# Three PSUM tiles that take turns from chunk to chunk, and an early copy of the fourth product

## The chip, the cores and the metric

The kernel runs on one core of one Trainium2 chip. The metric is the device time of one execution in microseconds (us); the time before is the median of three runs. The profile is of one further execution, whose own time is given beside its span.

The engines are called as the profile calls them: PE (matmuls), PEld (PE's weight loads, which overlap its matmuls), DVE, ACT, POOL, and SP, which only issues transfers.

## The reference, cut to what matters

One transformer block on `x` of 2048 tokens by 576, all in fp32:

```python
h  = x + attention(layernorm(x)) @ wo        # 32 heads of 18, window of 8 keys, dilation 2
n  = layernorm(h)
g  = n @ w_gate                              # 576 x 4608
u  = n @ w_up                                # 576 x 4608
out = h + (sigmoid(g) * u) @ w_down          # 4608 x 576
```

The change touches only the way in which `g` and `u` leave PSUM. What is computed stays the same.

## The kernel before, in words

**Blocks and chunks.** The tokens are cut into four blocks of 512. The 4608 columns of `w_gate` and `w_up` are cut into 36 chunks of 128. A product of one chunk is a PSUM tile of 128 columns by 512 tokens, which is one whole bank of 2 KB per partition. fp32 values are split into a high and a low part (`split`, lines 103 to 105: ACT copies the high part, DVE subtracts), and each product is made of three passes: high by high, weight high by operand low, weight low by operand high.

**Two ways to do a chunk.** A list of 86 items (line 971) is worked off in order. In the first way, `single` (line 644), one block's `g` and `u` are computed plainly with the PSUM tiles `b1` and `b2`. In the second, `pair` (line 671), two blocks are done together, and seven products take the place of eight (the scheme of Strassen and Winograd; the operands `s1` to `s4` and `t1` to `t4` are sums and differences made before). The order of items is: 14 `single` for block 0, 22 `pair` for blocks 0 and 1, 14 `single` for block 2, 36 `pair` for blocks 2 and 3. The text counts items from 0, so the first `pair` stage is items 14 to 35 and the second is items 50 to 85.

**One chunk of `pair`.** The seven products are called product 1 to product 7 here. A product is six matmuls with 512 columns (`prod`, line 604, matmuls on line 609), and products 2, 5, 6 and 7 have two more for the last 64 rows of the contraction (`rest`, line 613, matmuls on line 616).

| product | tile before | what follows it |
|---|---|---|
| 1: `a00` by `b00` | `b1`, fresh | ACT copies it to `s1` (line 676) |
| 2: `a01` by `b10` | `b2`, fresh | DVE adds it to `s1` (681), ACT takes the sigmoid (682): gate of the first block |
| 3: `s2` by `t2` | `b1`, added to product 1 | ACT copies the sum to `s2` (686) |
| 4: `s3` by `t3` | `b3`, fresh | nothing yet |
| 5: `s1` by `t1` | `b1`, added on | ACT copies the sum to `s3` (693), then DVE adds `b3` to `s3` (694): up of the second block |
| 6: `a11` by `t4` | `b3`, added to product 4 | DVE adds it to `s2` (699), ACT takes the sigmoid (700): gate of the second block |
| 7: `s4` by `b11` | `b1`, added on | `last`: DVE multiplies the first gate by `b1`, then the second gate by `s3` (line 629, or 1041 in the second pair stage) |

Product 6 writes on `b3` and so must come after line 694 has read it. Product 3 of each chunk must come after line 676, and product 5 after line 686. Product 1 of the next chunk takes `b1` afresh, and so must come after the multiplication by `b1`. `s1` to `s3` come from four buffers that take turns (`s_tile`, line 632).

**The other work of those stages.** `between(0)` to `between(6)` stand behind the products. They let in the down projection, which runs a few items behind: in the first pair stage 24 matmuls with 288 columns after products 5 and 7 (`down_units`, matmuls on line 719), in the second stage one step of six such matmuls after each product (`down_seven`, matmuls on line 781, each step's PSUM tile copied out by ACT on line 787 and added to DRAM by POOL's queue on line 790). The last four chunks go back to the plain scheme (`down_tail`, line 756). The first pair stage also has the attention of blocks 2 and 3 behind it, which is DVE work in pieces such as line 182. Weights are split one chunk ahead (`weights`, line 575).

**PSUM.** The eight banks are `b1`, `b2`, `b3`, `bgp`, and two tiles `dp` of two banks each, which take turns. The projections that run under the `single` items use `b3` and `bgp` (`bg_bank`, line 640).

**What sets the order.** Each engine works through its own list in order. The lists are made when the program is built, by a planner of the framework that simulates the engines with its own estimates. It takes the instruction that it thinks ready first, and among ready ones the one with the higher priority, then the one that was traced first. So the order on PE can differ from the program's text: where the planner thinks a product is blocked, it lets matmuls of the down projection go ahead. `tc.high_priority(HC)` raises the priority of the evictions (copies and adds that read PSUM). A new tile on a bank waits until every reader and writer of the tile before it is done.

Of the kernel before, what the change touches and what calls it, by code (L numbers as in the profile page):

```python
# [17 lines left out]
AF = mybir.ActivationFunctionType  # L18
ALU = mybir.AluOpType
# [34 lines left out]
HC = 700  # L54
# [6 lines left out]
def kernel(ctx, tc, x, wqkv, wo, wmlp, out):  # L61
    nc = tc.nc
    dve, act, pool, pe, sp = nc.vector, nc.scalar, nc.gpsimd, nc.tensor, nc.sync
# [540 lines left out]
    def prod(ps, xx, w, n, first):  # L604
        wt, k0 = w[n]
        k = 0
        for c in range(2):
            for a, m in ((0, 0), (0, 2), (1, 0)):
                pe.matmul(ps, wt[:, a, k0 + c], xx[:, m + c], start=first and k == 0,  # L609
                          stop=k == 5, skip_group_check=True)  # L610
                k += 1

    def rest(ps, xx, w, n):
        wt, k0 = w[n]
        for a in range(2):
            pe.matmul(ps, wt[:, a, k0], xx[:, 4], start=False, stop=a == 1,  # L616
                      skip_group_check=True)
# [14 lines left out]
    def s_tile():  # L632
        return gh.tile([P, TB], F32, tag="s", bufs=4, name="s")

    def b_tile(i):
        return gp.tile([P, TB], F32, name=f"b{i % 3 + 1}")
# [31 lines left out]
    added = [None]  # L668
    gated = [None]

    def pair(X, w, between, last):
        b1, b2, b3 = b_tile(0), b_tile(1), b_tile(2)
        s1, s2, s3 = s_tile(), s_tile(), s_tile()
        prod(b1, X["a00"], w, "b00", True)
        with tc.high_priority(HC):
            act.activation(s1, b1, AF.Copy)
        between(0)
        prod(b2, X["a01"], w, "b10", True)
        rest(b2, X["a01"], w, "g4")
        with tc.high_priority(HC):  # L680
            added[0] = dve.tensor_tensor(s1, s1, b2, ALU.add)
            act.activation(s1, s1, AF.Sigmoid)
        between(1)
        prod(b1, X["s2"], w, "t2", False)
        with tc.high_priority(HC):
            act.activation(s2, b1, AF.Copy)
        between(2)
        prod(b3, X["s3"], w, "t3", True)
        between(3)
        prod(b1, X["s1"], w, "t1", False)  # L690
        rest(b1, X["a11"], w, "u4")
        with tc.high_priority(HC):
            act.activation(s3, b1, AF.Copy)
            added[0] = dve.tensor_tensor(s3, s3, b3, ALU.add)  # L694
        between(4)
        prod(b3, X["a11"], w, "t4", False)
        rest(b3, X["a11"], w, "g4")
        with tc.high_priority(HC):
            added[0] = dve.tensor_tensor(s2, s2, b3, ALU.add)
            gated[0] = act.activation(s2, s2, AF.Sigmoid)  # L700
        between(5)
        prod(b1, X["s4"], w, "b11", False)
        rest(b1, X["s4"], w, "u4")
        with tc.high_priority(HC):
            last((s1, b1), (s2, s3))
        between(6)
# [253 lines left out]
    def units(n):  # L960
        for _ in range(n):
            while queue:
                if next(queue[0], END) is END:
                    queue.pop(0)
                else:
                    break
# [139 lines left out]
    for c, (kind, p, f) in enumerate(items):  # L1106
# [26 lines left out]
        def last(h0, h1):  # L1133
            hid[0] = hidden(*h0, "h0")
            hid[1] = hidden(*h1, "h1")
# [3 lines left out]
        elif not by_seven:  # L1139
            side = last_pair if c == NF - 1 else bg_step  # L1140

            def between(i):
                if i in (4, 6):
                    units(2)
                side(i)

            pair(X, w, between, last)
        else:
            def between(i):
# [12 lines left out]
                down_side(f, i)  # L1162

            pair(X, w, between, last if f >= NF - NPL else last_sums(f))
            if f < NF - NPL:
                if f % 2:
# [57 lines left out]
```

## Time and profile before

| what | us |
|---|---|
| time, median of three runs (lowest, highest) | 1599.83 (1598.15, 1600.38) |
| time of the profiled execution | 1598.48 |
| its span | 1596.1 |
| PE busy | 1561.0 (98% of the span) |
| weight loads | 1381.9 (87%) |
| DVE busy | 1269.6 (80%) |
| ACT busy | 875.3 (55%) |
| POOL busy | 184.0 (12%) |

The span lies between the first and the last instruction, and 2.4 us of the profiled execution's time lie around it. Busy time counts overlapping instructions once. Matmuls overlap, so a row of a matmul group shows a duration that is longer than the step from one matmul to the next; what one matmul costs is the step between starts. A wait of PE is shown twice: at the matmul, and at the weight load (PEld) ahead of it.

### The profile page before, as it was taken

Reading aid. Unit: us, or ns where it says so; the run is one execution under the profiler, and the core shown is the slowest. Engines: PE = TensorE matmul, PEld = TensorE weight load, DVE = VectorE, ACT = ScalarE, POOL = GpSimd, SP = SyncE. Lnnn points to the kernel's source line nnn. Section 1 sums busy time; section 2 is a strip of 40 time slices with the busy share of each in tenths; the row PEclk is TensorE's granted clock in tenths of the full one; section 3 lists DMA queues with packets and bytes.
Section 4 is the critical chain, followed back from the end, with each engine's and each line's share of the span. In section 5 each row is a group of like instructions: output and inputs, shape, how many; then the busy total and the mean of one; then the engine's idle time right before and its main releaser. Section 6 shows DMA issues by size and latency. Waiting matters only on the chain.

```text
span 1596.1 us, 22354 instructions
## 1 busy us (share of the span) xinstructions
PE 1561.0 (98%) x8532; PEld 1381.9 (87%) x8532; DVE 1269.6 (80%) x1931; ACT 875.3 (55%) x1546; POOL 184.0 (12%) x230
## 2 busy tenths in 40 slices
PE   7999979999999999999999999999999999999998
PEld 6999968798888888888989988888888888888887
DVE  7999989859999999999446777876777776677755
ACT  5432234435565566566443345766777776677751
POOL 1000000011000010001001100112112112211110
PEclk9999999999999999999999999999999999999999
DMA  7654544446466666666754234888888889888983
GB/s 270 205 203 168 187 183 165 154 162 247 112 167 186 163 161 168 169 176 153 200 185 164 78 111 123 186 182 177 170 171 188 175 168 183 172 167 181 187 166 123
DMA packets 76891, 273.50 MB, mean 171 GB/s; under 512 B 8336, under 2 KB 14224, under 8 KB 75888
## 3 DMA queue, kind: packets, MB, share of 16 engines
q0 software_dynamic: 27792, 105.89, 35.0%
q1 hardware_dynamic: 41360, 146.06, 27.8%
q10 hardware_dynamic: 7632, 20.12, 3.3%
q8 instruction: 67, 1.10, 0.3%
q14 instruction: 40, 0.33, 0.1%
HBM read 145.88 MB, written 128.52 MB: 172 GB/s over the span
## 4 chain that ended last, share of the span: by engine, by line
PE 83%; DVE 9%; DMA 4%; issue 1%; ACT 1%; POOL 0%; SPq 0%; DVEq 0%; POOLq 0%; ACTq 0%
PE b L609 40%; PE dp L719 14%; PE dp L781 11%; PE b L616 7%; PE acc L150 5%; DMA wg<-in_wmlp_dram 1%; PE b L150 1%; PE bgp L150 1%; DVE pr L182 1%; DVE pr L208 1%; DVE lg L186 1%; DVE w L105 1%; DMA x<-tok 1%; DVE tl L105 1%; DMA ar<-x 1%
## 5 line engine op out<-in xcount | busy, mean ns | idle before, releaser
L609 PE MATMUL b<-tl,w 128*128 128x512 f32 x1716 | 441.4, 396 | 8.7 <-ACT w L104 6.2
L609 PEld LDWEIGHTS b<-tl,w 128*128 128x128 f32 x1716 | 310.3, 189 | 68.8 <-ACT w L104 7.3
L609 PE MATMUL b<-th,w 128*128 128x512 f32 x1368 | 355.0, 394 | 1.0 <-DVE s L694 0.5
L609 PEld LDWEIGHTS b<-th,w 128*128 128x128 f32 x1368 | 248.7, 188 | 54.1 <-DVE s L694 4.7
L616 PE MATMUL b<-th,w 128*128 128x512 f32 x572 | 176.4, 390 | 0.0
L104 ACT ACTIVATE w<-wg 128x640 fp32r<-128x640 f32 (+2 forms) x197 | 116.5, 597 | 107.9 <-PE b L616 40.2
L790 POOL DMA_DIRECT2D h<-ev x128 | 110.1, 862 | 464.6 <-ACT ev L787 446.2
L787 ACT ACTIVATE ev<-dp 128x576 f32<-128x576 f32 x224 | 144.8, 647 | 34.0 <-PE dp L781 31.1
L150 PE MATMUL acc<-qw,th 128*128 128x432 f32 x512 | 155.8, 365 | 1.1 <-DVE th L109 0.8
L105 DVE TENSOR_TENSOR w<-wg,w 128x640 fp32r<-128x640 f32 (+2 forms) x197 | 126.6, 649 | 37.0 <-ACT w L104 36.7
L105 DVE TENSOR_TENSOR w<-tw,w 128x512 fp32r<-128x512 f32 x116 | 79.6, 687 | 70.0 <-ACT w L104 69.0
L616 PEld LDWEIGHTS b<-th,w 128*128 128x128 f32 x572 | 107.4, 188 | 22.7
L104 ACT ACTIVATE w<-tw 128x512 fp32r<-128x512 f32 x116 | 73.3, 632 | 91.1 <-PE b L609 85.7
L719 PE MATMUL dp<-d,h0h 128*128 128x288 f32 x640 | 119.3, 296 | 0.9 <-DVE tail L729 0.9
L719 PE MATMUL dp<-d,h1h 128*128 128x288 f32 x640 | 120.2, 297 | 0.0
L719 PEld LDWEIGHTS dp<-d,h0h 128*128 128x128 f32 x640 | 99.6, 190 | 5.0 <-DVE tail L729 1.2
L150 PEld LDWEIGHTS acc<-qw,th 128*128 128x128 f32 x512 | 97.2, 190 | 6.5 <-DVE th L109 1.1
L719 PEld LDWEIGHTS dp<-d,h1h 128*128 128x128 f32 x640 | 99.6, 190 | 2.9 <-ACT h1h L104 0.2
L150 PE MATMUL acc<-qw,tl 128*128 128x432 f32 x256 | 92.8, 362 | 0.0
L384 ACT ACTIVATE ev<-acc 128x432 f32<-128x432 f32 x64 | 33.9, 531 | 104.9 <-PE acc L153 101.7
L727 ACT ACTIVATE stage<-dp 128x576 f32<-128x576 f32 x96 | 61.8, 646 | 40.3 <-PE dp L719 40.0
L182 DVE TENSOR_TENSOR pr<-kw,q 128x2304 f32<-128x2304 f32 x32 | 81.7, 2552 | 2.7 <-DMA kw<-k 2.6
(278 smaller groups left out, 2904.5 us busy)
## 6 DMA issues: line engine op xcount, KB each, us to landing
h<-ev POOLq DMA_DIRECT2D x96, 576.0 KB, 7.0
wg<-in_wmlp_dram SPq DMA_DIRECT2D x49, 928.0 KB, 5.1
h<-stage POOLq DMA_DIRECT2D x24, 1152.0 KB, 11.1
wg<-in_wmlp_dram SPq DMA_DIRECT2D x36, 640.0 KB, 4.9
kw<-k SPq DMA_DIRECT2D x16, 792.0 KB, 4.3
vw<-v SPq DMA_DIRECT2D x16, 792.0 KB, 5.4
wd<-in_wmlp_dram SPq DMA_DIRECT2D x18, 576.0 KB, 6.6
h<-ev POOLq DMA_DIRECT2D x32, 288.0 KB, 6.1
```

Source lines behind the costliest of these rows:

```text
L104: act.activation(hi, src, AF.Copy)
L105: splits.append(dve.tensor_tensor(lo, src, f32(hi), ALU.subtract))
L150: pe.matmul(ps[:, :n], a[:, c, js], m[:, c], start=k == 0, stop=False)
L182: dve.tensor_tensor(pr, both(kw, u), q[:, us].unsqueeze(2).broadcast_to([P, 2, W, CG]), ALU.mult)
L384: act.activation(ev[:, :, j], ps[:, :NQ].rearrange("p (t c) -> p t c", t=3), AF.Copy)
L609: pe.matmul(ps, wt[:, a, k0 + c], xx[:, m + c], start=first and k == 0, stop=k == 5, skip_group_check=True)
L616: pe.matmul(ps, wt[:, a, k0], xx[:, 4], start=False, stop=a == 1, skip_group_check=True)
L719: pe.matmul(ps[:, i, :DH2], a[:, js], d[:, m, i * DH2:(i + 1) * DH2], start=k == 0, stop=k == n)
L727: act.activation(hv, ps, AF.Copy)
L781: pe.matmul(ps[:, i, :DH2], a[x][:, js], m[y], start=k in (0, 1, 3) and q == 0, stop=q == 2, skip_group_check=True)
L787: act.activation(hs[:, k % 2], ps[:, :, :DH2], AF.Copy)
L790: pool.dma_start(hsev[:, u, k0:k + 1], hs[:, :k + 1 - k0], accum_op=ALU.add, max_dma_last_dim=8 * D)
```

## The change: what it does

Before, `pair` always takes the tiles `b1`, `b2`, `b3` in this order. After, a counter `turn` goes up by one with each chunk, and the three tiles are taken from that place on: `b1, b2, b3`, then `b2, b3, b1`, then `b3, b1, b2`, and so on (`b_tile` takes its number modulo three). The names in the code keep their parts: what the code calls `b1` holds products 1, 3, 5 and 7.

Beside this the up sum of the second block is put together the other way round. Before, ACT copied the tile of products 1, 3 and 5 to `s3` after product 5, and DVE added the tile of product 4. After, ACT copies the tile of product 4 to `s3` as soon as product 4 is done, and DVE adds the tile of products 1, 3 and 5 after product 5. The number of instructions of each kind is the same.

```diff
+    turn = [2]
+
     def pair(X, w, between, last):
-        b1, b2, b3 = b_tile(0), b_tile(1), b_tile(2)
+        turn[0] += 1
+        b1, b2, b3 = (b_tile(turn[0] + k) for k in range(3))
         s1, s2, s3 = s_tile(), s_tile(), s_tile()
...
         prod(b3, X["s3"], w, "t3", True)
+        with tc.high_priority(HC):
+            act.activation(s3, b3, AF.Copy)
         between(3)
         prod(b1, X["s1"], w, "t1", False)
         rest(b1, X["a11"], w, "u4")
         with tc.high_priority(HC):
-            act.activation(s3, b1, AF.Copy)
-            added[0] = dve.tensor_tensor(s3, s3, b3, ALU.add)
+            added[0] = dve.tensor_tensor(s3, s3, b1, ALU.add)
         between(4)
         prod(b3, X["a11"], w, "t4", False)
```

## The prediction

> **What bounds the kernel now.** I read the page first, then PE's waits, then PE's busy time and clock by stage, and last the chain of waits and the timeline inside the second pair stage. From the page, and from the table of waits of PE over the whole span (total us, times, longest):
>
> ```profile
> span 1596.1 us, 22354 instructions
> PE 1561.0 (98%) x8532; PEld 1381.9 (87%) x8532; DVE 1269.6 (80%) x1931; ACT 875.3 (55%) x1546; POOL 184.0 (12%) x230
> ```
> ```profile
> PE bgp L139 <- DVE tl L105: 3.9, 1, 3.9
> PE b L609 <- DVE s L629: 2.9, 2, 2.5
> ...
> PE b L609 <- DVE s L694: 0.5, 1, 0.5
> ```
>
> PE is the bound, and the table shows one wait on line 694, of 0.5 us. By that table the change has almost nothing to win. But it lists gaps between matmuls only, and a late weight load hides in the matmul's own duration. The weight loads' waits inside the second pair stage (1009.77 to 1527.7 us), and the windows of PE's busy time (columns: window, its length, PE, PEld, DVE, ACT, POOL, PE clock, DMA share, GB/s):
>
> ```profile
> PEld b L609 <- DVE s L694: 2.9, 16, 0.2
> ```
> ```profile
> 819.50:826.30 6.80, 5.89 (x22) 5.37 (x23) 5.38 (x11) 4.69 (x11) 0.00 (x0) 0.50 0.39 146
> 1009.77:1527.70 517.93, 517.93 (x2760) 449.13 (x2759) 374.90 (x645) 369.74 (x646) 102.55 (x120) 1.00 0.89 179
> ```
>
> PE is busy for all of 517.93 us, yet 16 weight loads wait for line 694, some 0.2 us each. What such a wait costs is read from the pitch. The chain of waits in that stage (start, length, what) is PE alone, and repeats every 34.53 us, which is two chunks with the 14 steps of the down projection between:
>
> ```profile
> 1013.49 0.45 PE b L616 x2
> 1013.94 1.46 PE dp L781 x11
> 1015.40 1.60 PE b L609 x6
> 1017.01 0.45 PE b L616 x2
> 1017.46 0.13 PE dp L781
> 1017.59 1.37 PE b L609 x6
> 1018.96 0.45 PE b L616 x2
> 1019.41 0.94 PE dp L781 x7
> 1020.35 1.48 PE b L609 x6
> 1021.83 0.66 PE dp L781 x5
> 1022.50 1.37 PE b L609 x6
> ...
> 1031.32 1.59 PE dp L781 x12
> 1032.91 1.65 PE b L609 x7
> ...
> 1037.93 1.45 PE b L609 x6
> ...
> 1048.47 1.46 PE dp L781 x11
> ```
>
> Six undisturbed matmuls of line 609 take 1.37 us (product 7 at 1017.59, product 2 at 1022.50), so one costs 0.228; a matmul of line 781 costs 0.133 (1.46 by 11). Directly after down matmuls I allow 1.39 for six: 0.02 for the change of shape. Four pieces take longer than that. The one at 1015.40 is product 6, the one at 1020.35 the next chunk's product 1, the one at 1032.91 begins with product 6 of the second chunk, and the one at 1037.93 is product 1 of the chunk after. From the timeline of all engines, what these wait for:
>
> ```profile
> 1013.98 0.60 ACT L693 ACTIVATE s<-b 128x512 f32<-128x512 f32 x1 [1.19 <-PE b L616]
> ...
> 1014.61 0.69 DVE L694 TENSOR_TENSOR s<-s,b 128x512 f32<-128x512 f32 x1 [1.85 <-ACT s L693]
> ...
> 1015.35 1.22 PEld L609 LDWEIGHTS b<-th,w 128*128 128x128 f32 x6 [0.18 <-DVE s L694]
> ...
> 1019.45 0.69 DVE L1041 TENSOR_TENSOR r<-s,b 128x512 f32<-128x512 f32 x1
> ```
>
> Product 5 ends, ACT copies its tile, DVE then adds `b3`, and only at 1015.30 may product 6 write `b3`. PE had pulled five matmuls of the next down step forward (11 in a row at 1013.94, not 6) and still came too early. Likewise line 1041 reads `b1` until 1020.14, and product 1 at 1020.2 is the new tile on that bank.
>
> **The change part by part.**
>
> *The early copy.* No instruction is added or removed; the 0.60 us copy moves from product 5's end to product 4's, and the 0.69 us add stays where it was. Product 6 now waits for the copy of product 4's tile, which has all of product 5 and a down step as cover: 8 x 0.228 + 0.8 = 2.6 us against 0.60. So product 6's waits go. Per two chunks: 1.60 - 1.38 = 0.22 us, and 1.65 - 7 x 0.229 = 0.05.
>
> *What it newly makes late.* Product 7 adds to the tile that DVE now reads after product 5, so it waits for line 694. Its cover runs from product 5's end to product 7's start, 1013.94 to 1017.59 = 3.65 us in the rows, against 0.69 of add; DVE work of up to 2.9 us may stand ahead of the add before PE feels it. On ACT, the copy waits for product 4; behind it are queued evictions of the down projection and weight splits, which waited in the same way behind product 5 before, so this trades places and costs nothing while ACT keeps up (369.74 of 517.93 us busy). `s3` is held longer by some 2.6 us; its buffer was the last chunk's `s2`, whose last reader, the second multiplication of line 1041 right behind the one at 1019.45, is done three products before product 4 ends. No transfer moves; SP and POOL have the same lists.
>
> *The turn.* Product 1 now takes the bank that the last chunk's product 2 had, free since line 681, a whole half chunk earlier. Its wait for line 1041 goes: 1.48 - 1.39 = 0.09 and 1.45 - 1.39 = 0.06 per two chunks, call it 0.16 with rounding. Product 2 takes the bank that line 699 reads with an add like line 694's of 0.69 us right after product 6; from there to product 2 lie product 7, a down step and product 1, 1.82 + 0.8 + 1.37 = 4.0 us. Product 4 takes the bank of line 1041, later still. Nothing binds there.
>
> *Sum in the second stage.* 0.22 + 0.05 + 0.16 = 0.43 us per two chunks, with the rounding of the rows 0.40 to 0.48; I take 0.44. 32 of the 36 chunks carry the seven-product down projection (the table's 16 waits are one per two chunks): 16 x 0.44 = **7.0 us**. As an upper bound: two chunks have 100 matmuls of lines 609 and 616 and 14 x 6 = 84 of line 781, and 100 x 0.228 + 84 x 0.133 = 33.97 us of bare matmuls against the period of 34.53 leave 0.56, so no more than 9.0 us even if every change of shape became free.
>
> *First pair stage: nothing.* Its 22 chunks show no wait of these kinds, since a full down tile pair stands there after product 5 (these rows are from the chain over the whole span and from the page's groups):
>
> ```profile
> 395.33 3.18 PE dp L719 x24
> ```
> ```profile
> L182 DVE TENSOR_TENSOR pr<-kw,q 128x2304 f32<-128x2304 f32 x32 | 81.7, 2552 | 2.7 <-DMA kw<-k 2.6
> ```
>
> *The border to the second stage.* Items 50 on start at another place of the turn (22 chunks are one more than a multiple of three), so the first product there takes the bank that the last `single` used for its up product, not the long free one. Timeline:
>
> ```profile
> 957.77 0.62 PE L616 MATMUL b<-th,w 128*128 128x512 f32 x2
> ...
> 958.22 1.52 PE L609 MATMUL b<-tl,w 128*128 128x512 f32 x6
> ...
> 958.67 0.68 DVE L629 TENSOR_TENSOR s<-s,b 128x512 f32<-128x512 f32 x1
> ```
>
> Product 1 started at 958.22; now it must wait for 959.35, 1.1 us later, unless down matmuls go ahead of it. Between 0 and 1.1 us of loss, once; six such matmuls (0.8 us) are there, so I take 0.3.
>
> *The last chunk.* Product 6 waits there longest, because a tail add stands ahead of line 694 on DVE. Chain over the end, and timeline:
>
> ```profile
> 1555.76 8.43 DMA tail<-h
> ```
> ```profile
> 1563.50 1.67 PE L609 MATMUL b<-th,w 128*128 128x512 f32 x6 [0.50 <-DVE s L694]
> ...
> 1569.55 0.53 PE L719 MATMUL dp<-d,h0h 128*128 128x288 f32 x2 [0.91 <-DVE tail L729]
> ```
>
> The 0.8 us before product 6 go (0.50 and the uncovered load), but the end hangs on the tail's transfer and on the DVE adds behind it; PE only comes to its next wait, on line 729, earlier. Between 0 and 0.8; I take 0.
>
> *Sum.* 7.0 - 0.3 = 6.7 us. The profiled execution took 1598.48, so 1591.8 there. It lies 1.35 under the median of the runs, 1599.83, against which I set the forecast: **1593.1 us**.
>
> **The rivals.**
>
> *The planner re-orders and the loss comes back elsewhere.* The lists are made anew at build. In the old list the pulled-forward down matmuls show that the planner sees product 6 as blocked; without that its choice differs in each chunk, and evictions and splits on ACT and DVE move too. For it: the pieces of 7 and 5 matmuls of line 781 around 1020.35 show that the planner already cuts a step in two around a product. Against: the covers above are 2.6 us and more. If all 0.44 comes back, the time is 1599.8; if one of the two waits stays (product 6's part is 0.27 of 0.43, product 1's 0.16), the gain is 2.5 to 4.3, less 0.3: about 1596.5.
>
> *Slower: product 7 behind attention on DVE, in the first pair stage.* There DVE holds pieces of 2.55 us (line 182). Product 7 follows product 5 after 24 down matmuls and product 6, 3.18 + 1.82 = 5.0 us. One piece ahead of the add costs nothing (2.55 + 0.69 = 3.2); with two the add ends at 5.8 and PE loses 0.8 a chunk, 22 x 0.8 = 18 us: 1599.8 - 6.7 + 18 = 1611. It decides from 4.3 us of DVE work ahead of the add. Against: before, product 6 waited for the same add with 3.18 us of cover, and PE lost nothing there; the add has the evictions' priority. In part it could also hold a few chunks only; 9 chunks make it slower than before.
>
> *The clock.* After PE's 3.9 us wait for line 105 the granted clock was 0.50 from 819.5 to 826.3. A turn of the banks that made PE stop that often would cost 6.8 x 0.5 = 3.4 us each time, 58 times 197 us: 1790. Against it, the granted clock of the second stage is 1.00, and both `dp` tiles take turns in it already; I give it 1 in 100. The Trainium skill has such a rule in "TensorE: Matmul & The Clock Gate", section "A second HAM failure mode: psum-queue depth-cycling": a bf16 kernel whose PSUM use cycled through the banks each iteration idled briefly between matmul groups so often that the clock gate went to and fro. By that rule this change would be harmful; the row of 1.00 does not bear it out for cycling as such.
>
> **How the numbers follow.** The full gain, 1590.5 to 1595.5: 62 in 100. More than that (the bound of 9.0, the last chunk's 0.8): 4. Part of it, around 1596.5: 12. It comes back elsewhere, 1597.5 to 1602: 13. Slower, by product 7 or the clock or a worse list: 9. Two tenths of a per cent, 3.2 us, is about what runs of this kernel can tell from no change. Under 1596.6 lie 62 + 4 and two thirds of the 12: faster 0.74. Over 1603.0 lie 9, less a part of them that stays small: slower 0.09. Same 0.17. The range goes from 1589.5 (9.0 + 0.8 of gain, with rounding) to 1599.5, just under no change: it holds 62, 3, 12 and half of the 13.
>
> **What would show it.** In the second stage the period of two chunks should fall from 34.53 to about 34.1. The row of PEld's waits on line 694 should be gone, with none on 1041 in its place, and product 6 should take 1.39 after six down matmuls, not 11. The copy after product 4 (line 693 of the changed kernel) should start within 1 us of product 4's end, and PE should not wait for the add (its line 698) anywhere. The first pair stage should be as long as before. I am wrong if the period stays, if product 7 shows a wait for the add, or if the first pair stage or the items 36 to 50 get longer.

## The result

| kernel | median us (lowest, highest) | ratio to before (95% interval) |
|---|---|---|
| before, beside the first timing | 1599.38 (1598.15, 1600.38) | |
| changed | 1590.88 (1587.33, 1591.42) | 0.9944 (0.9928, 0.9960) |
| changed, timed once more | 1589.93 (1587.55, 1591.20) | 0.9943 (0.9929, 0.9957) |

The change makes the kernel faster by 8.5 us in the first comparison and 9.6 us in the second (against 1599.53); the interval of the second is 6.9 to 11.4 us. The forecast was 1593.1, a gain of 6.7 us. The profiled execution took 1591.42 against 1598.48. From the page of the changed kernel:

```profile
span 1589.2 us, 22383 instructions
PE 1553.3 (98%) x8532; PEld 1381.6 (87%) x8532; DVE 1268.1 (80%) x1931; ACT 869.2 (55%) x1546; POOL 184.2 (12%) x230
```

Every engine has as many instructions as before and much the same busy time, but for 7.7 us less on PE and 6.1 on ACT. PE's busy time contains its late weight loads, so its row shows the gain. Lines after `pair` have moved down by four (785 is the old 781), those inside it by three or four (679 is the old 676).

The chain of waits in the second pair stage, at the place shown of before (start, length, what; after 1019 it follows POOL's queue and no longer PE, mostly through pieces in which POOL waited for nothing that the profile shows, while PE has no gap in the stage):

```profile
1013.98 0.80 PE dp L785 x6
1014.77 1.39 PE b L609 x6
1016.16 0.46 PE b L616 x2
1016.63 0.79 PE dp L785 x6
1017.42 1.37 PE b L609 x6
```

Product 6, at 1014.77, comes after one down step and not after 11 matmuls, and takes 1.39 us instead of 1.60. Product 7 follows after the next step. The timeline around it, all engines:

```profile
1011.39 0.60 ACT L693 ACTIVATE s<-b 128x512 f32<-128x512 f32 x1 [0.73 <-PE b L609]
...
1014.01 0.69 DVE L698 TENSOR_TENSOR s<-s,b 128x512 f32<-128x512 f32 x1 [0.79 <-PE b L616]
...
1014.62 1.55 PE L609 MATMUL b<-th,w 128*128 128x512 f32 x6
...
1017.26 1.53 PE L609 MATMUL b<-th,w 128*128 128x512 f32 x6
```

The copy starts 0.2 us after product 4's six matmuls, within the 1 us that was forecast, and is done 2.6 us before product 6. The add ends at 1014.70, and product 7 begins at 1017.26. The same product 6 of the next two chunks starts 34.11 us later:

```profile
1048.73 1.55 PE L609 MATMUL b<-th,w 128*128 128x512 f32 x6
```

The table of PEld's waits of that stage (1010 to 1530 us) is empty now; it had 16 waits for line 694.

For the experiments, one measure is free of the noise at both ends: the time from the fifth to the 31st copy of product 1 in the second pair stage, which is 26 chunks or 13 periods. The first two rows are from the timeline of ACT of the kernel before, the last two of the changed kernel:

```profile
1021.89 0.59 ACT L676 ACTIVATE s<-b 128x512 f32<-128x512 f32 x1
...
1470.86 0.59 ACT L676 ACTIVATE s<-b 128x512 f32<-128x512 f32 x1
```
```profile
1021.86 0.58 ACT L679 ACTIVATE s<-b 128x512 f32<-128x512 f32 x1
...
1465.42 0.58 ACT L679 ACTIVATE s<-b 128x512 f32<-128x512 f32 x1
```

448.97 us became 443.56. All kernels by this measure, with the times of those that were run several times:

| kernel | 26 chunks, us | a period | median us | ratio to before |
|---|---|---|---|---|
| before | 448.97 | 34.54 | 1599.38 | |
| before, second trace | 449.72 | 34.59 | | |
| turn alone | 446.33 | 34.33 | 1593.14 | 0.9964 (0.9952, 0.9977) |
| early copy alone | 446.97 | 34.38 | 1594.77 | 0.9975 (0.9966, 0.9984) |
| changed | 443.56 | 34.12 | 1590.88 | 0.9944 (0.9928, 0.9960) |
| changed, second trace | 443.56 | 34.12 | 1589.93 | 0.9943 (0.9929, 0.9957) |
| turn set back at item 50 | 443.56 | 34.12 | | |
| three dependent adds | 443.56 | 34.12 | 1588.49 | 0.9935 (0.9920, 0.9949) |
| seven dependent adds | 443.65 | 34.13 | 1598.21 | 0.9996 (0.9986, 1.0006) |
| down steps in twos | 442.78 | 34.06 | 1588.06 | 0.9930 (0.9918, 0.9943) |

Here the changed kernel gives the same 443.56 in both traces, and the kernel before differs by 0.75 between its two. (The two kernels of one edit each, the second timing of the changed kernel and the down steps in twos were compared with a median of 1599.53 of the kernel before, the two kernels with added instructions with 1599.22.)

### The profile page after: what moved, and what is told of

Read it like the earlier page. It is cut to its first block, busy times and chain, and to the rows that moved or that the text cites. A ratio compares the mean times of both kernels' runs of the same rounds, so it can differ in the third digit from the quotient of the medians.

```text
span 1589.2 us, 22383 instructions
## 1 busy us (share of the span) xinstructions
PE 1553.3 (98%) x8532; PEld 1381.6 (87%) x8532; DVE 1268.1 (80%) x1931; ACT 869.2 (55%) x1546; POOL 184.2 (12%) x230
## 4 chain that ended last, share of the span: by engine, by line
PE 55%; issue 27%; POOL 7%; DVE 6%; DMA 4%; ACT 1%; SPq 0%; POOLq 0%; ACTq 0%; DVEq 0%
PE b L609 23%; PE dp L723 15%; POOL h L794 7%; PE acc L150 6%; PE b L616 4%; PE b L150 1%; PE bgp L150 1%; DMA wg<-in_wmlp_dram 1%; DVE pr L182 1%; DMA x<-tok 1%; DVE pr L208 1%; DVE lg L186 1%; PE acc L152 1%; DMA tail<-h 1%; PE acc L153 1%
```

## The experiments

The theory: the gain is the time of two waits that PE's weight loads hid, product 6's (removed by the early copy) and product 1's (removed by the turn). Rivals: the planner's new order is what pays; one wait only passes to the other; the add that product 7 now waits for has little cover.

**The changed kernel once more.**

> The changed kernel once more, as the yardstick for the others on the same chip. Theory (each removed wait is worth what its rows showed): 6.7 us under the kernel before, period of two chunks in the second pair stage 34.12 us against 34.53. Rival (part of the gain in the first comparison was a difference between executions outside the stage): 4 us or less.

Measured: period 34.12, and 9.6 us under before. The rival is out. The gain is above the theory's 6.7, which lies just outside this interval (6.9 to 11.4) and just inside that of the first comparison (6.4 to 11.5).

**The turn alone.**

```diff
+        turn[0] += 1
+        b1, b2, b3 = (b_tile(turn[0] + k) for k in range(3))
...
             act.activation(s3, b1, AF.Copy)
             added[0] = dve.tensor_tensor(s3, s3, b3, ALU.add)
```

> The kernel before with the turn of the three tiles alone; the copy and the add stay after product 5. Theory: product 1 no longer waits, product 6 still does. Period 34.53 - 0.16 = 34.37 us; time 16 x 0.16 - 0.3 = 2.3 us under before. PEld still has 16 waits for line 694's add (697 here), and the planner still pulls 5 or 6 steps of the down projection ahead of product 6. Rival (the even order of the list is what pays, and it needs both parts): period still 34.53, no gain.

Measured: period 34.33, so 0.20 a period against 0.16 expected. The table of PEld's waits from 1010 to 1530 us:

```profile
PEld b L609 <- DVE s L697: 3.2, 17, 0.2
```

Product 6's waits are all there (the 17th, at 1529.55, is the next one of the series), and the uneven order ahead of it too; the rival is out. In time it is 6.4 us under before by the medians (interval 3.7 to 7.7), more than the 2.3 expected; of the 4.7 us by which its span is shorter than that of before, 2.6 lie in the 26 chunks, 1.0 behind them, and 0.7 between the two pair stages, where this execution had a shorter stretch at half clock (the last section has its size) and the change does nothing.

**The early copy alone.**

```diff
-        turn[0] += 1
-        b1, b2, b3 = (b_tile(turn[0] + k) for k in range(3))
+        b1, b2, b3 = b_tile(0), b_tile(1), b_tile(2)
```

> The kernel before with the early copy of the fourth product alone; the tiles stay b1, b2, b3. Theory: product 6 no longer waits, product 1 still does. Period 34.53 - 0.27 = 34.26 us; time 16 x 0.27 = 4.3 us under before; no wait of PEld for the add. Rival (the two are one wait: what product 6 doesn't lose, product 1 loses): period over 34.4, gain under 2 us.

(The diff is against the changed kernel.) Measured: period 34.38, a gain of 0.15 and not 0.27; 4.8 us under before by the medians (interval 2.6 to 5.4). No wait for the add is left, as the theory says, but product 1 waits longer than before. The timeline of DVE of the kernel before, then those of DVE and PE of this one, at the same place of the stage:

```profile
1123.05 0.69 DVE L1041 TENSOR_TENSOR r<-s,b 128x512 f32<-128x512 f32 x1
1123.66 0.68 DVE L1041 TENSOR_TENSOR r<-s 128x512 f32<-128x512 f32 x1
```
```profile
1120.59 0.69 DVE L1044 TENSOR_TENSOR r<-s 128x512 f32<-128x512 f32 x1
1121.20 0.68 DVE L1044 TENSOR_TENSOR r<-s,b 128x512 f32<-128x512 f32 x1
```
```profile
1121.76 0.30 PE L784 MATMUL dp<-d,s1h 128*128 128x288 f32 x1
1121.93 1.65 PE L609 MATMUL b<-tl,w 128*128 128x512 f32 x6
```

In the kernel before, line 1041 first read `b1` and then multiplied the two SBUF tiles. With the early copy, `s3` is ready sooner, and here the multiplication of `s2` by `s3`, which reads no PSUM, stands ahead of the one that frees the bank. The bank is free at 1121.88 and product 1 starts at 1121.93. Counted from the end of product 7, the bank comes free 0.03 us later than before in this chunk and 0.17 later in the next.

The steps between matmul starts, averaged over the 26 chunks, give the sum of a period. Against the same pieces of the changed kernel, product 6 and the step ahead of it cost 0.25 us more in the kernel before and nothing here. Product 1 and the step ahead of it cost 0.19 more in the kernel before and 0.27 here. And PE changes once more to the down projection and back (14 groups of down matmuls a period, 13 before), which costs 0.01 to 0.02 (six matmuls take 1.39 behind down matmuls and 1.37 behind others; the next run gives 0.01). That makes 0.25 - 0.08 - 0.02 = 0.15, as measured: a third of what product 6 no longer loses, product 1 loses, and the rival is right in part. In the changed kernel the two multiplications also stand in this order, and it costs nothing, since product 1 takes another bank: 0.25 + 0.19 - 0.02 = 0.42, as measured. This also answers the rival of the planner's new order, as far as changes of shape go: the changed kernel too has 14 groups a period, one more than before.

**The down steps in twos.**

```diff
-                units(1)
+                units((2, 0, 2, 0, 2, 0, 1)[i] if f % 2 == 0 else (0, 2, 0, 2, 0, 2, 1)[i])
```

> The changed kernel with the 14 steps of the down projection let in two at a time in the second pair stage, so that PE changes between 512 and 288 columns 16 times per two chunks, not 28 times. Theory (what is left over the bare matmuls in the changed kernel, some 0.26 us per two chunks, is the change of shape, 0.02 us for each way there and back): period 34.12 - 6 x 0.019 = 34.01 us, time 1.8 us under the changed kernel. Rival (the leftover is in the matmuls themselves): period 34.12. Second rival (two steps in a row make PE wait for the eviction of a down tile): period over 34.2, slower than the changed kernel.

Measured: period 34.06. Half of the 0.11 that was expected came; so the change of shape is a part of what is left over the bare matmuls, and 0.01 for each way there and back in place of 0.019. Why these six gave only half of it, no run shows. No wait for a down tile showed. Its median, 1588.06, is 1.9 us under the changed kernel's in the same comparison, but the two intervals overlap, so it is the period alone that shows it faster.

**The kernel before once more.**

> The kernel before once more, for a second trace of it. Theory: the stretches outside the pair stages (the half-clock stretches near 232 and 820 us, the end after the last product 1) differ between executions of one kernel by 1 to 3 us, while the period of 34.53 us does not. Rival: they are the same as in the first trace, so what the changed kernel gained there is the change's own.

Measured: 1598.26 us, period 34.59. Outside the pair stages the two traces differ by 0.4 us (up to the first copy of product 1), 0.8 (between the stages) and 0.7 (the end), less than the 1 to 3 of the theory; and the period does differ, by 0.06. The wait has a spread of its own from execution to execution; without it (changed kernel) the spread of the period is gone.

**The turn set back at item 50.**

```diff
         if c == NF + NSTD:
+            turn[0] = 2
             finish_bg()
```

> The changed kernel with the turn set back at item 50, so that the second pair stage begins with the long free bank as before. The prediction's border term: 0.3 us faster than the changed kernel in the first four chunks of the stage. Rival (the planner lets down matmuls go ahead and nothing is lost there): the first four chunks take the same, within 0.1 us.

Measured: from the last product 1 of the first pair stage to the fifth of the second, 264.80 us (756.78 to 1021.58), against 264.70 and 264.72 in the two traces of the changed kernel, and 266.05 and 265.29 before. The half-clock stretch near 820 us lies in this time, and it was one step longer in the first trace of before. Free of it is the time from the last gate sigmoid of the `single` items (ACT, line 653) to the same copy: 67.52 with the turn set back, 67.61 and 67.58 in the changed kernel, 68.25 and 68.32 before. The rival holds: starting on the bank that was just used costs 0.06 to 0.09 us in the sum, not 0.3. The wait itself exists. Timeline of PE of the changed kernel, at the first product 1:

```profile
959.62 0.40 PE L609 MATMUL b<-th,w 128*128 128x512 f32 x1
960.01 1.66 PE L609 MATMUL b<-tl,w 128*128 128x512 f32 x6
```

The step of 0.39 is 0.16 longer than a matmul's 0.23, and the six that follow take 1.50 and not 1.39: 0.26 or so in all, near the 0.3 that was taken for it. The kernel with the turn set back has no such wait and gains at most a third of its price: its product 1 stands at another place of the list, ahead of the down matmuls and not behind them.

**Three, and seven, dependent instructions on the tile that product 7 writes.**

```diff
             added[0] = dve.tensor_tensor(s3, s3, b1, ALU.add)
+            if c >= NF + NSTD:
+                for _ in range(3):
+                    dve.tensor_tensor(s3, s3, b1, ALU.subtract)
+                    added[0] = dve.tensor_tensor(s3, s3, b1, ALU.add)
```

(This is the kernel with seven; the one with three has the two lines once.)

> The changed kernel; in the second pair stage the tile of products 1, 3 and 5 is added to s3, taken off and added again, so that DVE has three dependent instructions on that tile after product 5 where it had one (same result but for rounding, 1.2 us more DVE work a chunk). Theory (product 7 has over 3 us of cover, so the add costs nothing): period stays at 34.12 us within 0.05, time as the changed kernel within 2 us. Rival (product 7 is close behind the add, or DVE's work as a whole decides): period 34.12 + 2 x 0.5 us or more, time 10 us or more over the changed kernel.

> The same with seven dependent instructions (3.7 us more DVE work a chunk), some 4.4 us after product 5 before product 7 may write. Theory (the cover is about 3.4 us: a down step, product 6 and a down step): it is used up, product 7 waits for the last add in each chunk, by 0.2 us if the planner lets one more down step ahead and by 1 us if not: 7 to 36 us slower than the changed kernel. Rival (the planner's freedom covers it all): same as the changed kernel within 2 us.

Measured with three: the period is 34.12 to the hundredth, and the time is not above the changed kernel's. The add does cost nothing, with room for two more. Measured with seven: the period is 34.13, so the rival holds in the stage, though DVE is busy for 487.14 of 520 us there:

```profile
1010.00:1530.00 520.00, 519.49 (x2805) 454.69 (x2804) 487.14 (x838) 374.00 (x655) 105.81 (x123) 1.00 0.93 181
```

(Columns: window, length, PE, PEld, DVE, ACT, POOL, PE clock, DMA share, GB/s.) How it is covered, PE's timeline shows, with the last of the seven instructions on DVE behind it:

```profile
1119.91 1.55 PE L609 MATMUL b<-th,w 128*128 128x512 f32 x6
...
1123.35 1.55 PE L609 MATMUL b<-tl,w 128*128 128x512 f32 x6
...
1125.53 2.90 PE L609 MATMUL b<-th,w 128*128 128x512 f32 x12
```
```profile
1125.77 0.68 DVE L702 TENSOR_TENSOR s<-s,b 128x512 f32<-128x512 f32 x1
```

After product 6 (1119.91) the planner issues two down steps and then product 1 of the next chunk (1123.35, the `a00` operand), and after a third down step the 12 matmuls of two products. The first six of these are product 2 of the next chunk: the last of the seven instructions ends at 1126.45, and product 7 is the second six, from 1126.91. So two products of the next chunk go ahead of it. Its product 1 can, because with the turn it no longer takes the bank of product 7. The 10 us by which this kernel is slower than the kernel with three adds lie elsewhere: in the last chunks and the tail (129.45 us from the 31st copy to the end, against 121.30), where DVE's backlog ends in a wait of PE, and in the first four chunks (2.3 us more). So the 8.3 us by which it is slower than the changed kernel lie in the theory's range of 7 to 36 by chance: the place where the theory put them, a wait of product 7 in each chunk, shows none. Its waits of PE after 1530 us (the copy of line 689 had itself waited 4.8 us for a multiplication on DVE):

```profile
PE b L609 <- ACT s L689: 2.4, 1, 2.4
PE dp L727 <- DVE tail L737: 1.4, 2, 0.8
```

## Why the prediction was right, and where its sizes were off

**The bound and the hidden wait: right.** PE's matmul rows showed 0.5 us of waits on line 694; the pitch showed 0.43 a period. 0.42 of it is gone by the first two traces, and 0.47 against the second trace of before. For the 16 periods that the prediction counted that is 6.7 to 7.6 us, against 7.0. The count itself was read a little wrong: the 517.93 us of its table are 15 periods, and the 16 waits are one in each and a second in the last, where the pattern of two chunks ends. 13 of the 16 lie in the 26 chunks, one before them and two behind.

**The split between the two edits: off.** The prediction gave product 6's wait 0.27 and product 1's 0.16. Alone, the early copy brought 0.15 and the turn 0.20, and together 0.42, which is 0.06 more than their sum. By the steps the two waits were 0.25 and 0.19, close to what the prediction gave them; the step that failed is the one that cost the moved copy at nothing beside its own wait. It also makes `s3` ready sooner, and with that the order of the two multiplications on DVE changes (0.08 a period, alone), and it gives PE one more change of shape (0.02). With the turn the first is harmless, so the total did not suffer. That the planner changes the order because `s3` is ready sooner is the likely reason; no run shows its choice by itself.

**The covers: right.** Product 7 has 3.45 us from product 5's end at 1013.81 to 1017.26 (forecast 3.65), and three dependent instructions fit into it. The sign that PE should not wait for the add anywhere failed once: in the first trace of the changed kernel product 7 of the last chunk waits 0.3 us for it (shown below), behind an add of the tail on DVE; in the second trace it does not. The rival on the slower side (product 7 behind attention in the first pair stage) did not come about: from its first to its last copy of product 1 that stage took 366.14 us against 366.08.

**The border: price right, sum not.** The wait was 0.26 us, for 0.3 forecast. But the time from the last `single` sigmoid to the fifth chunk of the second stage became 0.6 to 0.7 us shorter (68.25 and 68.32 to 67.61 and 67.58), where the prediction had 0.1: one of the 16 periods less 0.3. What it left out are the first chunks, where the down projection does not yet stand between all products. PEld's waits for evictions from 960 to 1010 us, before (the same in its second trace) and then changed (its second trace has none):

```profile
PEld b L609 <- ACT s L693: 0.4, 2, 0.2
PEld b L609 <- ACT s L676: 0.3, 1, 0.3
PEld b L609 <- ACT s L686: 0.3, 1, 0.3
PEld b L609 <- DVE s L694: 0.2, 1, 0.2
```
```profile
PEld b L609 <- DVE s L629: 0.3, 1, 0.3
```

With the turn alone this time is 67.94, and with the early copy alone 68.27: here, too, the two edits together are worth more than their sum.

**The end: taken as nothing, was a gain of 0.8 to 3.2 us with the periods in it.** From the 31st copy to the end 125.28 and 124.62 us became 123.79 and 122.04. Two of the 16 periods lie in it, 0.9 us, and were counted. The end hangs, as the prediction said, on the tail's load from DRAM and the adds behind it: a run of 168 down matmuls that takes 22.6 us in each of these traces comes after them. The loads are issued 1.2 to 1.5 us earlier after the 31st copy than before. The rest of the difference is how long they take, which changes from execution to execution. The chain over the end, in the first and the second trace of the changed kernel:

```profile
1549.04 8.24 DMA tail<-h
```
```profile
1548.16 6.70 DMA tail<-h
```

As forecast, what product 6 no longer loses in the last chunk mostly goes to the next wait, on the eviction of the tail. Waits of PE after 1530 us in the first trace of the changed kernel:

```profile
PE dp L723 <- DVE tail L733: 1.7, 1, 1.7
PE b L609 <- DVE s L698: 0.3, 1, 0.3
```

In its second trace the wait on line 733 is 0.6 and the other is gone, and its end is 1.75 us shorter than that of the first: so much does the end differ between executions of one kernel.

**The sum.** By the traces the gain is 5.4 to 6.2 us in the 26 chunks (5.7 forecast), 0.6 to 0.7 in the first ones (0.1 forecast) and 0.8 to 3.2 at the end (0.9 forecast): 6.9 to 10.1 in all, which holds both 8.5 and 9.6. So the shortfall of 6.7 lies in the first chunks, for certain, and in the end, where the change's part and the spread of executions can't be told apart further with these runs.

**The clock: the rival is out.** The granted clock of the stage is 1.00, with all banks taking turns:

```profile
1009.80:1527.70 517.90, 517.90 (x2794) 453.40 (x2793) 372.27 (x643) 369.92 (x652) 104.27 (x122) 1.00 0.92 180
```

The rule of "TensorE: Matmul & The Clock Gate" of the Trainium skill (section "A second HAM failure mode: psum-queue depth-cycling") speaks of short idle times between groups of matmuls; this turn leaves none (PE busy for 517.90 of 517.90 us), and the trace does not show the effect.

## What to carry to other kernels

A PE that is busy for the whole of a stage can still lose time to semaphores: a weight load that comes late is shown as a longer first matmul, so compare the pitch of equal groups of matmuls along the stage, and look at the weight loads' own waits. Where an accumulator bank is written afresh by one iteration while the last one's reader still works, letting the banks take turns cost nothing in this stage and gave the planner freedom besides: with seven dependent instructions on the tile it put the next two products ahead of the blocked one. And an eviction that is moved earlier makes its consumer ready earlier too; if that consumer shares an in-order queue with the reader that frees a bank, the two may change places.

## What the runs showed that was not expected

A weight load that waits for a semaphore costs PE more than the late start. Timeline of PE of the kernel before, product 6 and product 7:

```profile
1015.35 1.66 PE L609 MATMUL b<-th,w 128*128 128x512 f32 x6
...
1016.85 0.61 PE L616 MATMUL b<-th,w 128*128 128x512 f32 x2
...
1017.43 1.53 PE L609 MATMUL b<-th,w 128*128 128x512 f32 x6
...
1018.80 0.61 PE L616 MATMUL b<-th,w 128*128 128x512 f32 x2
```

Once begun, product 6's six matmuls take 1.50 us here and 1.39 in the changed kernel. The 0.11 come on top of the late start, which is another 0.11 (the down matmul ahead of it takes 0.24 to the next start, not 0.13). They fit the load's own rows: product 6's first load and its first matmul both begin at 1015.35, while product 7's load begins at 1017.30 and its matmul at 1017.43, so that there the load lies 0.13 under the matmul before. That the unhidden load is the whole of the 0.11 is an inference.

The half-clock stretches differ between executions of one kernel. Around 820 us the windows of the two traces of the kernel before give a mean clock of 0.57 and 0.79 over 8 us:

```profile
819.00:827.00 8.00, 6.59 (x26) 5.89 (x27) 6.45 (x12) 5.19 (x12) 0.00 (x0) 0.57 0.45 160
```
```profile
819.00:827.00 8.00, 5.93 (x28) 5.21 (x29) 6.55 (x12) 6.07 (x14) 0.00 (x0) 0.79 0.46 170
```

That is 6.9 us at half clock in the one and 3.4 in the other, a difference of one step of 3.4 us. The Trainium skill's "TensorE: Matmul & The Clock Gate", section "Part 1: The HAM clock gate (the "warmup" mystery)", states a free-running window of 3413 ns, and the length of these stretches agrees with it; that the window runs freely, no run here shows. A step at half clock would cost up to 1.7 us of PE work by its length, an estimate; between these two traces, the time from the last product 1 of the first pair stage to the fifth of the second differs by 0.8. Near 232 us it went the other way: from 231 to 247 us the mean clock is 0.68 in both traces of the kernel before and 0.57 in both of the changed one, where the first product 1 of the first pair stage comes 0.4 to 1.3 us later. Kernels with the changed `pair` and added work later on show the shorter stretch there, so it is not the change. Such a step is as large as several of the terms that the prediction summed.
